# First batch of an attention-and-experts kernel: row sums from a second, crosswise product, and its last two head pairs side by side

## The chip, the cores and the metric

The kernel runs on one NeuronCore of a Trainium2 chip. The metric is the device time in microseconds (us) of one execution, median of several runs. An engine's work is issued in program order on that engine's own queue: TensorE (PE) multiplies and transposes, VectorE (DVE) and ScalarE (ACT) do elementwise work, GpSimd (POOL) does slower elementwise work, and SyncE (SP) issues the DMA transfers.

## What is computed

Three layers follow each other over 8 batches of 576 tokens with 8 heads of 64 (512 columns a token):

```python
kv  = einsum('bhsd,bhse->bhde', k, v)          # per head 64 x 64
out = einsum('bhsd,bhde->bhse', q, kv)
x   = out / sqrt(mean(out*out, -1) + 1e-6) * g_norm     # per head
xn  = x / sqrt(mean(x*x, -1) + 1e-6) * rms_g            # per token
y   = (silu(xn @ w_gate) * (xn @ w_val)) @ w_out        # 512 -> 1536 -> 512
# then: each token goes to the best of 8 experts (512 -> 1024 -> 512)
```

The scale of a token therefore needs, for each of its 8 heads, the sum of the squares of `out` over 64 columns, and the same sum weighted with g_norm squared.

## The kernel before, in words

The order of the work is written out by hand: the program's order is the order on each engine's queue, and waits between engines follow from the data. The work comes in nine chunks of 512 tokens (chunk 0 is the first 512 tokens of batch 0). In chunk 0 the gated layer is also fed: its float64 weights are loaded as pairs of 32-bit words and turned into float32 and then into a high and a low part (class `Convert`: `rebias` L909 on ACT, `narrow` L922, L923, L926 on DVE, `high` L949 on ACT, `low` L959 on DVE). A raw weight buffer comes free for the next load when `narrow` is through.

The change lies in the opening, L1470 to L1509, ahead of the first product of the gated layer. Heads go in four pairs. For each pair of batch 0:
- `column` (L672) copies k or q into an order with the token in the partition; k's copies are on DVE, q's on ACT.
- `kv` (L678) multiplies k and v (20 products of 64 columns a pair, L691) and copies the two 64 x 64 blocks of the result into `kvb`, one on DVE (L692), one on ACT (L693).
- `turn` (L695) transposes q on PE (four transposes, L703); ACT copies the result out of PSUM (L705).
- `av` (L708) makes four products of 128 columns (L715): tokens in the partitions, the pair's 128 columns along the row. ACT squares it (L719) and copies it to `xo` (L720); POOL multiplies the squares with g squared (`sg`, L737); DVE sums both over 64 columns (L741, one for the squares, one for `sg`).

`finish` (L757) turns the sums into a scale per token and head with seven small DVE instructions (L761 to L767), `root` (L771) takes the square root on ACT, ACT then loads the table for Silu (L1504), `scale` (L775) scales `xo` for one head pair at a time on DVE (L777), and `tstep` (L840) transposes it (L844), makes the high part on ACT (L848) and the low part on DVE (L849). The products of the gated layer (L154 to L156) start with the first of them.

In the opening, pairs 0 and 1 are loaded alone, pairs 2 and 3 together (`krest`, `vrest`, `qrest`), and behind them on SP's queue come four weight loads, with g_norm (`gcol`, L127 and L128) and rms_g between the first and the second, and then batch 1. The pairs are taken one after the other (L1478 to L1488). While DVE and ACT end the batch, PE does 56 transposes of the identity that nobody reads (L1498 and L1499).

Of the kernel before, what the change touches and what calls it, by code (L numbers as in the profile page):

```python
# [10 lines left out]
F32 = mybir.dt.float32  # L11
F32R = mybir.dt.float32r
# [3 lines left out]
ALU = mybir.AluOpType  # L16
# [4 lines left out]
P = 128  # L21
# [44 lines left out]
def attention_moe_kernel(ctx, tc, q, k, v, g_norm, w_gate, w_val, w_out, rms_g, wg2, w1, w2, out):  # L66
# [267 lines left out]
    class Block:  # L334
# [47 lines left out]
        def turn(self, t):  # L382
            m = self.rows[t]
            ps = ptile(f"tr{self.nm}_{t}")
            for kk in range(KD):
                nc.tensor.transpose(
                    ps[:, kk * P : kk * P + m], self.xg[t][:m, kk * P : kk * P + P], ident[:m, :m]
                )
            p3 = ps.rearrange("p (k t) -> p k t", k=KD)[:, :, :m]
            sl = slice(t * P, t * P + m)  # L390
            if not self.slots:
                split(self.whole[0][:, :, sl], self.whole[1][:, :, sl], p3)
                return
            for i in range(2):
                split(self.xh[i][:, :, sl], self.xl[i][:, :, sl], p3[:, 2 * i : 2 * i + 2])
# [218 lines left out]
    class Attention:  # L614
# [54 lines left out]
                    q[self.b - 1 + i, :, 512:S, :].rearrange("h s d -> s h d"),  # L669
                )  # L670

        def column(self, nm, hp, copy=nc.scalar.copy):  # L672

            t = att.tile([P, 4, 2, HD], F32, tag="col", bufs=2, name=f"{nm}c{self.b}_{hp}")
            copy(t, self.t[hp][nm].rearrange("p h j d -> p j h d"))
            self.col[nm, hp] = t.rearrange("p j h d -> p j (h d)")

# [14 lines left out]
            nc.vector.tensor_copy(kb[0:64, h0 : h0 + n, 0:64], pt[0:64, 0:n, 0:64])  # L692
            nc.scalar.copy(kb[64:128, h0 : h0 + n, 64:128], pt[64:128, 0:n, 64:128])  # L693

        def turn(self, hp):  # L695
            self.sums()
            ps = self.ps(f"qT{self.b}_{hp}")
            for j in range(4):
                if hp < 4:
                    src = self.col["q", hp][:, j, :]  # L700
                else:
                    src = x5[:, 2 * j : 2 * j + 2, :].rearrange("p h d -> p (h d)")
                nc.tensor.transpose(ps[:, j * P : j * P + P], src, ident)  # L703
            qT = att.tile([P, 4, P], F32, tag="qT", bufs=2, name=f"qTs{self.b}_{hp}")
            nc.scalar.copy(qT.rearrange("p a b -> p (a b)"), ps)  # L705
            self.qTs.append(qT)

        def av(self, hp, apart=False):  # L708
# [48 lines left out]
        def finish(self):  # L757
            self.sums()
            n = self.n
            a1, a2, m2 = s1[:, :n, :], s2[:, :n, :], st[:, :n]  # L760
            nc.vector.tensor_scalar(a1, a1, 1.0 / HD, EPS, op0=ALU.mult, op1=ALU.add)  # L761
            nc.vector.reciprocal(a1, a1)
            nc.vector.tensor_tensor(a2, a2, a1, op=ALU.mult)
            nc.vector.tensor_reduce(m2, a2, axis=AX.X, op=ALU.add)
            nc.vector.tensor_scalar(m2, m2, 1.0 / D, EPS, op0=ALU.mult, op1=ALU.add)
            nc.vector.reciprocal(m2, m2)
            nc.vector.tensor_tensor(  # L767
                a1, a1, m2[:, :, None].to_broadcast([P, n, 8]), op=ALU.mult
            )
# [20 lines left out]
        def steps(self, nxt, tight=False):  # L790


            def kv(h):
                self.kv(h, h + 1)
                for hp in (h, h + 1):
                    self.column("q", hp)
                if h == 0:
                    self.load(2, 3)
                else:
                    if self.n == 5:  # L800
                        self.load_last()
                    if nxt:
                        nxt.load(0, 1)

            def turn(h):
                for hp in (h, h + 1):
                    self.turn(hp)
                for hp in (0, 1):
                    if h == 0:
                        self.column("k", hp + 2)  # L810
                    elif nxt:
                        nxt.column("k", hp)

            def av(h):
                for hp in (h, h + 1):
                    self.av(hp, tight)

            res = []
            if self.b == 1:
                res += [idle, lambda: self.column("k", 0), lambda: self.column("k", 1), idle]  # L820
            for h in (0, 2):
                for f, kind in ((kv, "p"), (turn, "p"), (av, "a")):
                    res += [mark(kind, lambda f=f, h=h: f(h)), idle]
                if tight:
                    res[-1] = mark("v", lambda: self.squares())
            if self.n == 5:
                res += [mark("p", lambda: self.turn(4)), idle]
                res += [mark("a", lambda: self.av(4, tight)), idle]
                if tight:
                    res[-1] = mark("v", lambda: self.squares())  # L830
            res += [idle] * (1 if tight else 2)
            res += [mark("f", self.finish), idle, mark("t", self.root)]
            if self.n == 5:
                res.append(mark("v", self.scale_last))
            step = 2 if tight else 1
            for kk in range(0, KD, step):
                res.append(mark("v", lambda kk=kk: [self.scale(kk + i) for i in range(step)]))
            return res

    def tstep(c, kk):  # L840

        ps = (otile if (c, kk % 2) == (0, 1) else ptile)(f"xT{c}_{kk}")
        for j in range(4):
            nc.tensor.transpose(ps[:, j * P : j * P + P], xo[:, j, kk * P : kk * P + P], ident)  # L844
        if kk == 3:
            live[0] -= xt[kk] is not None
        x = (rslot if c < SINGLE and kk < 3 else wslot)(f"x{c}_{kk}")
        nc.scalar.activation(x[:, 0:512], ps, AF.Copy, scale=comb[:, kk : kk + 1])  # L848
        nc.vector.scalar_tensor_tensor(  # L849
            x[:, 512:1024], ps, comb[:, kk : kk + 1], x[:, 0:512].bitcast(F32),  # L850
            op0=ALU.mult, op1=ALU.subtract,
        )
        xt[kk] = x
# [621 lines left out]
    small_loads()  # L1475
    for _ in range(3):
        conv.load()
    for hp in range(4):  # L1478
        a0.column("k", hp, vec)
        if hp == 1:  # L1480
            nc.vector.tensor_tensor(g2b, g2b, g2b, op=ALU.mult)
        if hp > 1:
            a0.av(hp - 2)
        a0.column("q", hp)
        a0.kv(hp)
        if hp == 3:
            conv.rebias()
        a0.turn(hp)  # L1488
    a1.load(0, 1)
    late_loads()  # L1490
    conv.narrow()
    a0.av(2)
    a0.av(3)
    conv.high()
    conv.rebias()

    unread = otile("unread")
    for i in range(56):  # L1498
        nc.tensor.transpose(unread[:, 0:P], ident, ident)  # L1499
    a0.finish()  # L1500
    nc.vector.tensor_scalar(comb, comb, gcol[:, 0:1], None, op0=ALU.mult)
    conv.low()
    a0.root()
    nc.scalar.activation(warm, warm, AF.Silu)  # L1504
    for kk in range(KD):
        a0.scale(kk)
    tstep(0, 0)
    tstep(0, 1)
    conv.narrow()  # L1509

    def tstep_kk(kk):
# [704 lines left out]
```

## Time and profile before

| | us |
|---|---|
| median of 3 runs | 1455.35 |
| lowest and highest | 1452.74 and 1456.58 |
| the profiled execution | 1455.73 |
| its span, first to last instruction | 1454.1 |

The profile follows one execution. Times in it count from the start of the span. A row of the timeline has start, duration, engine, line, operation, what is written and read, the count, and in brackets how long the engine stood idle before it and what released it. "PEclk" is the share of TensorE's full clock that was granted (1.00 is 2.4 GHz, 0.50 is 1.2 GHz). Busy times of PE are modelled from pipelined instructions; a mean of one can be longer than its pace in a row of equal ones.

### The profile page before, as it was taken

The page shows a single profiled execution, that of the slowest core. Times are in us where ns is not written, and L with a number is a line of the kernel's source. Part 1 is how long each engine was busy: PE and PEld are TensorE (multiplying, and loading weights), DVE is VectorE, ACT ScalarE, POOL GpSimd, SP SyncE. Part 2 cuts the span into 40 slices and gives each one's busy share as a digit, 9 for nine tenths or more (in the row PEclk, how much of TensorE's full clock was granted, in tenths as well). Part 3 has the DMA queues.
Part 4 walks back from the last instruction along what each step waited for, and adds up shares of the span by engine and source line. Part 5 has one row for each costly group of instructions (what it writes and reads, how often), then busy time and mean ns, then how long its engine had stood idle before and what let it go on. Part 6 is the DMA issues. An engine that isn't in the chain of part 4 may idle for free.

```text
span 1454.1 us, 21584 instructions
## 1 busy us (share of the span) xinstructions
PE 1422.5 (98%) x7844; PEld 1196.3 (82%) x7844; DVE 928.9 (64%) x1970; ACT 629.8 (43%) x1173; POOL 198.5 (14%) x207
## 2 busy tenths in 40 slices
PE   6999999999999999999999999999999999999997
PEld 5776778888888888887888888788999989988985
DVE  5989675695677554665557446844462778578661
ACT  4655433433444544344222332243333556556651
POOL 2010001011012010101000100121404212302111
PEclk9999999999999999999999999999999999999999
DMA  7776856665666686558657555764323334424320
GB/s 218 247 220 215 277 167 173 212 219 152 209 212 177 204 272 192 174 167 280 241 191 212 178 190 198 219 213 122 131 81 99 106 127 141 134 93 134 119 84 30
DMA packets 162860, 255.55 MB, mean 176 GB/s; under 512 B 27331, under 2 KB 93123, under 8 KB 162752
## 3 DMA queue, kind: packets, MB, share of 16 engines
q1 hardware_dynamic: 131264, 190.26, 41.1%
q10 hardware_dynamic: 23040, 44.05, 9.4%
q0 software_dynamic: 8448, 19.85, 4.1%
q8 instruction: 63, 1.03, 0.3%
q14 instruction: 45, 0.37, 0.1%
HBM read 199.68 MB, written 55.30 MB: 175 GB/s over the span
## 4 chain that ended last, share of the span: by engine, by line
PE 85%; DVE 6%; DMA 5%; issue 3%; ACT 1%; SPq 1%; POOL 0%; POOLq 0%; ACTq 0%; DVEq 0%
PE A L1258 8%; PE X L1258 6%; PE po L154 6%; PE po L155 6%; PE po L156 6%; PE pv L154 3%; PE pv L155 3%; PE pv L156 3%; PE pg L154 3%; PE pg L155 3%; PE pg L156 3%; PE av L715 1%; PE kv L691 1%; DMA k<-in_k 1%; PE qT L703 1%
## 5 line engine op out<-in xcount | busy, mean ns | idle before, releaser
L1023 DVE SCALAR_TENSOR_TENSOR junk<-x,wgb 128x512 bf16<-128x512 f32 x256 | 183.0, 715 | 5.0
L154 PE MATMUL po<-wo,ahl 128*128 128x512 f32 x408 | 161.0, 395 | 0.9 <-DVE x L1001 0.9
L155 PE MATMUL po<-wo,ahl 128*128 128x512 f32 x408 | 159.0, 390 | 0.0
L156 PE MATMUL po<-wo,ahl 128*128 128x512 f32 x408 | 159.0, 390 | 0.0
L1258 PE MATMUL A<-xp,r 128*128 128x512 f32 x504 | 130.4, 394 | 1.9 <-DVE X L1834 1.3
L1258 PEld LDWEIGHTS A<-xp,r 128*128 128x128 f32 x504 | 93.1, 188 | 22.5 <-DVE X L1834 2.2
L737 POOL TENSOR_TENSOR sg<-sq,g2b 128x512 f32<-128x512 f32 x36 | 48.9, 1359 | 421.5 <-ACT sq L719 348.5
L1096 POOL DMA_INDIRECT idxd<-rec,si x36 | 38.3, 1064 | 458.6 <-DVE cs L1105 347.9
L1258 PE MATMUL X<-xp,r 128*128 128x512 f32 x360 | 93.3, 394 | 0.2 <-ACT X L1825 0.2
L154 PEld LDWEIGHTS po<-wo,ahl 128*128 128x128 f32 x408 | 76.6, 188 | 17.2 <-DVE x L1001 1.4
L156 PEld LDWEIGHTS po<-wo,ahl 128*128 128x128 f32 x408 | 76.6, 188 | 16.3
L155 PEld LDWEIGHTS po<-wo,ahl 128*128 128x128 f32 x408 | 76.7, 188 | 15.4
L1258 PEld LDWEIGHTS X<-xp,r 128*128 128x128 f32 x360 | 66.4, 188 | 14.8 <-ACT X L1825 0.9
L154 PE MATMUL pv<-x,wv 128*128 128x512 f32 x192 | 76.8, 400 | 0.7 <-DVE sl L1895 0.7
L154 PE MATMUL pg<-x,wg 128*128 128x512 f32 x192 | 77.1, 402 | 0.1
L155 PE MATMUL pg<-x,wg 128*128 128x512 f32 x192 | 75.2, 391 | 2.0 <-DVE wg L959 2.0
L155 PE MATMUL pv<-x,wv 128*128 128x512 f32 x192 | 75.4, 392 | 1.1 <-DVE wv L959 1.1
L156 PE MATMUL pg<-x,wg 128*128 128x512 f32 x192 | 75.1, 391 | 0.9 <-DVE x L849 0.9
L156 PE MATMUL pv<-x,wv 128*128 128x512 f32 x192 | 75.0, 391 | 0.0
L1896 ACT ACTIVATE ahl<-sl 128x512 fp32r<-128x512 f32 x42 | 26.5, 631 | 103.1 <-DVE sl L1895 100.2
L250 ACT ACTIVATE wo<-re 128x512 fp32r<-128x512 f32 x84 | 51.1, 627 | 31.8 <-DVE re L261 31.2
L253 DVE TENSOR_TENSOR wo<-re,wo 128x512 fp32r<-128x512 f32 x84 | 56.5, 684 | 9.5 <-ACT wo L250 9.1
(813 smaller groups left out, 3377.8 us busy)
## 6 DMA issues: line engine op xcount, KB each, us to landing
wo<-wos SPq DMA_DIRECT2D x90, 512.0 KB
r<-wst ACTq DMA_DIRECT2D x72, 512.0 KB
re<-in_moe_w SPq DMA_DIRECT2D x64, 512.0 KB
x1d<-x SPq DMA_DIRECT2D x32, 256.0 KB
k<-in_k SPq DMA_DIRECT2D x30, 256.0 KB
v<-in_v SPq DMA_DIRECT2D x30, 256.0 KB
q<-in_q SPq DMA_DIRECT2D x30, 256.0 KB
rg<-in_moe_w_gate SPq DMA_DIRECT2D x12, 512.0 KB
```

Of the source, the lines that this page charges most:

```text
L154: nc.tensor.matmul(ps, lhi, rhi, start=first, stop=False)
L155: nc.tensor.matmul(ps, llo, rhi, start=False, stop=False)
L156: nc.tensor.matmul(ps, lhi, rlo, start=False, stop=last)
L250: nc.scalar.activation(w[:, 0], part(n), AF.Copy)
L253: nc.vector.tensor_tensor(w[:, 1], part(n), w[:, 0].bitcast(F32), op=ALU.subtract)
L691: nc.tensor.matmul(pt[o, c, o], kj, vj, start=j == 0, stop=j == 4)
L703: nc.tensor.transpose(ps[:, j * P : j * P + P], src, ident)
L737: nc.gpsimd.tensor_tensor(sg, sq3, g2b[:, None, :].to_broadcast([P, 8, HD]), op=ALU.mult)
L1023: nc.vector.scalar_tensor_tensor(j, self.rows[t], 1.0, wgb[e], op0=ALU.mult, op1=ALU.mult, accum_out=self.L[:, t, e : e + 1],)
L1096: nc.gpsimd.indirect_dma_start(out=idxd[:], out_offset=bass.IndirectOffsetOnAxis(ap=si[:, j : j + 1], axis=0), in_=rec[:, j, :], in_offset ...
L1258: nc.tensor.matmul(ps, w[:, a, kk, :], x[kk][b], start=first and kk == j == 0, stop=kk == 1 and j == 2, skip_group_check=True,)
L1896: nc.scalar.activation(ahl[:, 0:512], sl, AF.Copy)
```

## The change

A class `Early` takes over the end of batch 0. For each pair, `across` makes the same product a second time the other way round: one product of 512 columns with the pair's 128 columns in the partitions and the tokens along the row. ACT squares that. `sums` multiplies the squares, 128 tokens at a time, by a 128 x 4 matrix `sel` (two columns of ones, two of g_norm squared, one of each for each head), so that TensorE makes both sums for both heads and leaves them in PSUM (`S`). `along` is the old product, copied to `xo` by ACT. `weigh` builds `sel` on POOL from `gcol`. DVE's sums (L741) and POOL's `sg` (L737) are gone from batch 0; the other batches keep them.

Pairs 2 and 3 are taken together: both columns of k, then q of pair 2 on DVE and of pair 3 on ACT, one `kv` for both, then `turn` for 2 (copied out by ACT) and for 3 (copied out by DVE). They have buffers of their own (`more`, `turned`). The unread transposes go from 56 to 6. `conv.low` moves from ahead of the root to behind the first `scale`, and scales 1 to 3 are issued between the steps of `tstep`.

```diff
--- before.py
+++ after.py
@@ -669,9 +669,10 @@
                     q[self.b - 1 + i, :, 512:S, :].rearrange("h s d -> s h d"),
                 )
 
-        def column(self, nm, hp, copy=nc.scalar.copy):
-
-            t = att.tile([P, 4, 2, HD], F32, tag="col", bufs=2, name=f"{nm}c{self.b}_{hp}")
+        def column(self, nm, hp, copy=nc.scalar.copy, t=None):
+
+            if t is None:
+                t = att.tile([P, 4, 2, HD], F32, tag="col", bufs=2, name=f"{nm}c{self.b}_{hp}")
             copy(t, self.t[hp][nm].rearrange("p h j d -> p j h d"))
             self.col[nm, hp] = t.rearrange("p j h d -> p j (h d)")
 
@@ -692,7 +693,7 @@
             nc.vector.tensor_copy(kb[0:64, h0 : h0 + n, 0:64], pt[0:64, 0:n, 0:64])
             nc.scalar.copy(kb[64:128, h0 : h0 + n, 64:128], pt[64:128, 0:n, 64:128])
 
-        def turn(self, hp):
+        def turn(self, hp, copy=nc.scalar.copy, qT=None):
             self.sums()
             ps = self.ps(f"qT{self.b}_{hp}")
             for j in range(4):
@@ -701,8 +702,9 @@
                 else:
                     src = x5[:, 2 * j : 2 * j + 2, :].rearrange("p h d -> p (h d)")
                 nc.tensor.transpose(ps[:, j * P : j * P + P], src, ident)
-            qT = att.tile([P, 4, P], F32, tag="qT", bufs=2, name=f"qTs{self.b}_{hp}")
-            nc.scalar.copy(qT.rearrange("p a b -> p (a b)"), ps)
+            if qT is None:
+                qT = att.tile([P, 4, P], F32, tag="qT", bufs=2, name=f"qTs{self.b}_{hp}")
+            copy(qT.rearrange("p a b -> p (a b)"), ps)
             self.qTs.append(qT)
 
         def av(self, hp, apart=False):
@@ -757,10 +759,15 @@
         def finish(self):
             self.sums()
             n = self.n
-            a1, a2, m2 = s1[:, :n, :], s2[:, :n, :], st[:, :n]
+            a1, a2 = s1[:, :n, :], s2[:, :n, :]
             nc.vector.tensor_scalar(a1, a1, 1.0 / HD, EPS, op0=ALU.mult, op1=ALU.add)
             nc.vector.reciprocal(a1, a1)
             nc.vector.tensor_tensor(a2, a2, a1, op=ALU.mult)
+            self.means()
+
+        def means(self):
+            n = self.n
+            a1, a2, m2 = s1[:, :n, :], s2[:, :n, :], st[:, :n]
             nc.vector.tensor_reduce(m2, a2, axis=AX.X, op=ALU.add)
             nc.vector.tensor_scalar(m2, m2, 1.0 / D, EPS, op0=ALU.mult, op1=ALU.add)
             nc.vector.reciprocal(m2, m2)
@@ -836,6 +843,64 @@
             for kk in range(0, KD, step):
                 res.append(mark("v", lambda kk=kk: [self.scale(kk + i) for i in range(step)]))
             return res
+
+    class Early:
+
+
+        def __init__(self, a):
+            self.a, self.q = a, []
+            self.sel = cpool.tile([P, 4], F32, name="gsel")
+            self.S = psg.tile([P, 512], F32, tag="v", name="S0")[:, 0:64].rearrange(
+                "p (j h i) -> p j h i", j=4, h=4
+            )
+            nc.gpsimd.memset(self.sel, 0.0)
+
+        def weigh(self):
+            for i in range(2):
+                o = slice(64 * i, 64 * i + 64)
+                nc.gpsimd.memset(self.sel[o, i : i + 1], 1.0)
+                nc.gpsimd.tensor_tensor(
+                    self.sel[o, 2 + i : 3 + i], gcol[o], gcol[o], op=ALU.mult
+                )
+
+        def across(self, hp):
+            qT = self.a.qTs[hp]
+            ps = ptile(f"aT{hp}")
+            nc.tensor.matmul(
+                ps, kvb[0][:, hp, :], qT.rearrange("p a b -> p (a b)"), start=True, stop=True
+            )
+            sq = att.tile([P, D], F32, tag="tmp", bufs=3, name=f"sqT{hp}")
+            nc.scalar.activation(sq, ps, AF.Square)
+            self.q.append(sq)
+
+        def sums(self, hp):
+            for j in range(4):
+                nc.tensor.matmul(
+                    self.S[:, j, hp, :], self.q[hp][:, j * P : j * P + P], self.sel,
+                    start=True, stop=True,
+                )
+
+        def along(self, hp):
+            qT, ps = self.a.qTs[hp], otile(f"av0_{hp}")
+            for j in range(4):
+                nc.tensor.matmul(
+                    ps[:, j * P : j * P + P], qT[:, j, :], kvb[0][:, hp, :], start=True, stop=True
+                )
+            nc.scalar.copy(
+                xo[:, 0:4, hp * P : hp * P + P], ps.rearrange("p (j e) -> p j e", e=P)
+            )
+
+        def finish(self):
+            a1, a2 = s1[:, 0:4, :], s2[:, 0:4, :]
+            p1, p2 = (
+                t.rearrange("p j (h i) -> p j h i", i=2) for t in (a1, a2)
+            )
+            nc.vector.tensor_scalar(
+                p1, self.S[:, :, :, 0:2], 1.0 / HD, EPS, op0=ALU.mult, op1=ALU.add
+            )
+            nc.vector.reciprocal(a1, a1)
+            nc.vector.tensor_tensor(p2, self.S[:, :, :, 2:4], p1, op=ALU.mult)
+            self.a.means()
 
     def tstep(c, kk):
 
@@ -1475,37 +1540,61 @@
     small_loads()
     for _ in range(3):
         conv.load()
-    for hp in range(4):
+    early = Early(a0)
+    for hp in range(2):
         a0.column("k", hp, vec)
         if hp == 1:
             nc.vector.tensor_tensor(g2b, g2b, g2b, op=ALU.mult)
-        if hp > 1:
-            a0.av(hp - 2)
         a0.column("q", hp)
         a0.kv(hp)
-        if hp == 3:
-            conv.rebias()
         a0.turn(hp)
+    early.weigh()
+    more, turned = (
+        wpool.tile([P, 1024], F32R, tag="w", bufs=NSLOT, name=f"more{i}").bitcast(F32)
+        for i in range(2)
+    )
+    more = more.rearrange("p (c j h d) -> p c j h d", c=2, j=4, h=2)
+    turned = turned.rearrange("p (c j t) -> p c j t", c=2, j=4)
+    a0.column("k", 2, vec)
+    a0.column("k", 3, vec, more[:, 0])
+    early.across(0)
+    early.along(0)
+    early.across(1)
+    a0.column("q", 2, vec)
+    a0.column("q", 3, t=more[:, 1])
+    a0.kv(2, 3)
+    a0.turn(2, qT=turned[:, 0])
+    early.sums(0)
+    early.sums(1)
+    conv.rebias()
+    a0.turn(3, vec, turned[:, 1])
     a1.load(0, 1)
     late_loads()
     conv.narrow()
-    a0.av(2)
-    a0.av(3)
+    early.across(2)
+    early.across(3)
+    early.along(1)
+    early.sums(2)
+    early.sums(3)
     conv.high()
     conv.rebias()
+    early.along(2)
+    early.along(3)
 
     unread = otile("unread")
-    for i in range(56):
+    for i in range(6):
         nc.tensor.transpose(unread[:, 0:P], ident, ident)
-    a0.finish()
+    early.finish()
     nc.vector.tensor_scalar(comb, comb, gcol[:, 0:1], None, op0=ALU.mult)
-    conv.low()
     a0.root()
     nc.scalar.activation(warm, warm, AF.Silu)
-    for kk in range(KD):
-        a0.scale(kk)
+    a0.scale(0)
+    conv.low()
+    a0.scale(1)
     tstep(0, 0)
+    a0.scale(2)
     tstep(0, 1)
+    a0.scale(3)
     conv.narrow()
 
     def tstep_kk(kk):
```

## Rows read from the trace of the kernel before

**Rows 1.** The page's part 4: shares of the chain that ended last, by engine.
```profile
PE 85%; DVE 6%; DMA 5%; issue 3%; ACT 1%; SPq 1%; POOL 0%; POOLq 0%; ACTq 0%; DVEq 0%
```

**Rows 2.** Busy time by stretch: stretch, length, engines (instructions), clock, DMA share, GB/s.
```profile
32.00:41.50 9.50, 7.42 (x33) 5.01 (x33) 9.30 (x18) 5.79 (x11) 0.00 (x0) 1.00 0.31 99
41.50:79.00 37.50, 37.48 (x229) 28.20 (x230) 32.60 (x56) 24.11 (x46) 3.10 (x3) 1.00 0.78 250
```

**Rows 3.** The chain in order of time, up to 90 us: start, us, what.
```profile
7.70 10.19 DMA rg<-in_moe_w_gate
...
50.73 1.32 PE kv L691 x40
...
81.97 7.85 DMA rw<-in_moe_w_out
```

**Rows 4.** Timeline, 11 to 17 us: a load issued, and two loads' first readers.
```profile
11.32 0.83 SPq L128 DMA_DIRECT2D gcol<-in_g_norm  x1
...
13.24 0.43 DVE L675 COPY kc<-krest 128x512 f32<-128x512 f32 x1 [1.95 <-DMA krest<-in_k]
...
16.25 0.62 ACT L675 COPY qc<-qrest 128x512 f32<-128x512 f32 x1 [1.68 <-DMA qrest<-in_q]
```

**Rows 5.** Timeline, 21 to 26 us: the last pair is turned; ACT behind it.
```profile
21.36 0.65 PE L703 MATMUL qT<-ident,qc 128*128 128x128 f32 x4 [0.58 <-ACT qc L675]
...
22.27 0.58 ACT L705 COPY qTs<-qT 128x512 f32<-128x512 f32 x1
...
23.00 0.60 ACT L719 ACTIVATE sq<-av 128x512 f32<-128x512 f32 x1
...
25.60 0.69 ACT L909 ACTIVATE cmv<-rv 128x512 f32<-128x512 f32 x1
```

**Rows 6.** Timeline, 27 to 37 us: from the sums to the gated layer.
```profile
27.36 0.19 DVE L761 TENSOR_SCALAR s<-s 128x32 f32<-128x32 f32 x1
...
28.95 0.23 DVE L1501 TENSOR_SCALAR comb<-comb,gcol 128x4 f32<-128x4 f32 x1
29.06 0.23 ACT L773 ACTIVATE s<-s 128x32 f32<-128x32 f32 x1 [2.78 <-DVE s L767]
...
29.31 1.28 ACT L1504 ACT_TABLE_LOAD   x1
29.69 2.49 DVE L777 TENSOR_TENSOR xo<-xo,s 128x512 f32<-128x512 f32 x4
...
31.86 0.19 PEld L154 LDWEIGHTS pg<-x,wg 128*128 128x128 f32 x1 [0.35 <-ACT x L848]
...
33.42 0.41 DVE L922 TENSOR_SCALAR cmv<-cmv 128x512 int32<-128x512 int32 x1
...
35.20 1.40 DVE L849 SCALAR_TENSOR_TENSOR x<-xT,comb,x 128x512 fp32r<-128x512 f32 x2
```

**Rows 7.** Groups by line and shape, 0 to 32 us: count | busy us, mean ns | idle.
```profile
L1499 PE MATMUL unread<-ident 128*128 128x128 f32 x56 | 6.3, 273 | 0.0
...
L737 POOL TENSOR_TENSOR sg<-sq,g2b 128x512 f32<-128x512 f32 x4 | 5.5, 1365 | 16.7 <-ACT sq L719 15.0 <-issue 1.6
...
L741 DVE TENSOR_REDUCE s<-sq 128x8 f32<-128x512 f32 x4 | 2.7, 684 | 4.0 <-ACT sq L719 4.0
...
L122 POOL CAST kw<-kw8i 128x32 f32<-128x32 int32 x1 | 0.2, 219 | 0.1
```

**Rows 8.** Groups of DVE by line and shape over the whole span.
```profile
L1001 DVE COPY x<-po 128x512 f32<-128x512 f32 x18 | 12.2, 687 | 14.2 <-PE po L156 14.1
```

**Rows 9.** The chain again: eight products of 512 columns in float32, at 47 us.
```profile
47.29 3.43 PE po L1942 x8
```

**Rows 10.** Busy time by stretch around the falls of the clock, columns as in rows 2.
```profile
13.60:17.00 3.40, 0.88 (x21) 0.78 (x22) 1.90 (x5) 1.69 (x4) 1.27 (x1) 1.00 1.08 306
17.00:20.40 3.40, 3.40 (x26) 3.18 (x28) 0.06 (x1) 1.37 (x4) 0.00 (x0) 0.50 1.01 323
...
24.00:30.40 6.40, 6.18 (x57) 5.94 (x55) 5.51 (x16) 3.58 (x7) 3.93 (x10) 1.00 0.96 193
```

## The prediction

> **What bounds the kernel now.** I read the chain of waits first. Over the whole span it is 85% PE [rows 1], but the change touches only the first 37 us, so that stretch decides. By stretches [rows 2], from 32.0 to 41.5 us DVE is busy 9.30 of 9.50 us and PE 7.42: the gated layer starts under DVE, which makes both x's low parts and the weights. From 41.5 to 79 us PE is full (37.48 of 37.50). No transfer in these stretches has a fixed hour: each weight load waits for a raw buffer that DVE's `narrow` frees, so an earlier start moves all of it forward. What has a fixed hour are the opening's loads, which SP issues from the first microsecond. krest is there at 13.24 us and qrest at 16.25 [rows 4]; the first weights, rg, at 7.70 + 10.19 = 17.89 us [rows 3].
>
> After qrest the old opening is a row of steps: two pairs after one another, PE at half clock from 17.0 to 20.4 [rows 10], the last pair turned at 21.36 and copied by 22.85 [rows 5], then its squares, POOL's last `sg`, a last sum, and `finish` from 27.36. Root at 29.06, scales from 29.69, the first gated product's weights at 31.86, `narrow` from 33.42, the last two low parts from 35.20 [rows 6]. `narrow` at 33.42 is the mark to beat: from there DVE has no gap worth the name.
>
> **What is removed.** Eight sums at 0.68 us on DVE and four `sg` at 1.37 us on POOL [rows 7]. Only the last `sg` and the last sums were on the path. The 50 transposes that go are 50 x 6.3/56 = 5.6 us of PE that nobody waits for; they cost time only through the clock (below).
>
> **The new opening, step by step.** Where the same instruction stands in the trace, its duration is used.
> - kv of pairs 2 and 3: 40 products in a row take 1.32 us [rows 3]; with krest copied twice by about 14.1 and vrest between krest and qrest (about 14.7), they end by 16.5. q is then last: DVE copies pair 2 from 16.25 in 0.43 (k's copy [rows 4]), ACT pair 3 in 0.62. So kv of pair 3 leaves the path.
> - turn of pair 2: 16.7 to 17.35 (0.65 [rows 5]), ACT's copy to about 17.95.
> - **`sums` of pairs 0 and 1** stand next on PE, ahead of turn 3, and need `sel`, which needs `gcol`. Its second half was issued at 11.32 [rows 4], behind rg on the same queue. If the queue lands in order, it comes after 17.89: I take 18.2. POOL's two last small instructions at 0.2 (the 128x32 cast takes 0.22 [rows 7]) give 18.6. PE, in order, waits from 17.35 to 18.6 with turn 3 queued behind: a new wait of 1.25 us. Bounds: no wait at all, if these few bytes overtake rg; upwards, gcol's first reader stands at 28.95 [rows 6], and POOL's instructions can't cost more than the 1.37 us of a `sg` [rows 7]. Rg's end is the nearer row, since it lies just ahead on the same queue.
> - One `sums` instruction pair (load 128 columns, multiply 4): no such shape is shown. An unread transpose goes at 6.3/56 = 0.11 us [rows 7] and has the same load; I take 0.11, between 0.03 (a 64-column kv product, 1.32/40) and 0.19 (one LDWEIGHTS [rows 6]). Eight: 0.9, to 19.5.
> - turn 3 to 20.15; DVE copies it out of PSUM. Price: 0.69, a copy of that size from PSUM [rows 8]; done 20.9.
> - `across` is one product of 512 columns, 3.43/8 = 0.43 us [rows 9]. Pair 2's hides in front of that copy; pair 3's is out by 21.55. ACT squares it until 22.2 (0.6, like the copies of rows 5). `along` 1 and the first four `sums` lie beside that; the last four add 0.45: `S` is ready at 22.85.
> - DVE's `narrow` (1.86 us, 33.42 to 35.28 [rows 6]) is queued ahead of `finish`, but starts at 20.9 and ends at 22.75. It costs nothing; without that cover `finish` would wait for it.
> - `finish` to root takes 29.06 - 27.36 = 1.70 [rows 6]; its operands now come partly from PSUM, which I price at nothing to 0.2. Root could start at 24.55. On ACT, `high` stands ahead of it and waits for `narrow` (22.75), with `rebias` and two copies of `xo` behind it. ACT's five starts after 23.00 reach 25.60, a pace of 0.52 [rows 5]: four from 22.8 end near 24.9 to 25.0, so root goes at **25.0**, against 29.06: 4.1 us earlier.
> - Behind the root some is given back. The first product stood 31.86 - 29.06 = 2.8 us behind the root [rows 6]; now scale 0 no longer waits for `low`, and the table load (1.28) with the first high part (0.7) sets it: about 27.4, 2.4 us behind. On DVE, however, `low` is no longer in the root's shadow, and DVE waits about 0.3 us for that high part. Scale 0 at 25.3, then `low`, scale 1 (2.49/4 = 0.62 each scale, 0.7 a low part [rows 6]) to 27.2, the wait to 27.5, then low part, scale, low part, scale give `narrow` at **30.15**. PE's two transposed blocks and ACT's high parts lie beside that.
>
> Sum: 33.42 - 30.15 = **3.3 us**. The weights need nothing earlier than they land: batch 1's loads and the first four weights stay on the same SP queue in the same order. 1455.73 of the profiled execution less 3.3 is 1452.4; the median is 0.4 lower, so 1452.0. Bounds of the single terms: `sel` on time gives 1.25 more; dearer `sums` (0.19) take 1.0 of it; ACT's tail (0.45) may or may not count. I hold a gain of 2.0 to 4.4 likely.
>
> **Rivals.**
> 1. *The clock falls.* From 13.6 to 17.0 PE was busy 0.88 of 3.40 us, and from 17.0 to 20.4 the granted clock was 0.50, that is 1.2 GHz; with the 56 unread transposes PE was busy 6.18 of 6.40 us from 24.0 to 30.4, at 1.00 [rows 10]. In the new opening PE has little to do from about 24.3 (6 unread transposes) to 27.4. A like fall there lasts 3.4 us if it is as long as that one, and delays PE by at most half of it, 1.7; DVE's queue covers part. Time: up to 1453.7. For it: the gap. Against: two transposed blocks lie in it, and DVE, not PE, sets the pace behind it [rows 2]. Chance 0.12. The Trainium skill, TensorE: Matmul & The Clock Gate, on the HAM clock gate, says that the throttled clock is the default and that an idle stretch brings it back, which speaks against taking the 50 transposes out; by that rule the time is this rival's, and the trace agrees that the clock falls after a thin stretch.
> 2. *The opening is shorter than summed.* gcol is four bytes a row and may land before rg's last part, and then turn 3 goes at 17.35. That gives 3.3 + 1.25, 1450.8; its first reader at 28.95 [rows 6] doesn't tell. Chance 0.24.
> 3. *The gain is absorbed.* The chain passes a weight load of 7.85 us at 81.97 [rows 3]; such a load met by other traffic could take the gain back. Against: it is itself released by DVE, so it comes earlier too. Time 1455. Chance 0.08.
> 4. *Slower: PE stands before `sums`.* Everything of pair 3 is queued behind that wait. It gives the whole gain back if `sel` comes 3.3 us later than summed, at 21.9. Four POOL instructions at the price of a `sg`, 1.37 [rows 7], behind 18.2 end at 23.7: 1.8 slower than before, 1457.2. With gcol as late as its first reader allows (28.95) and POOL cheap, `sel` would come 10.8 later, 7.5 slower than before: 1462.9. Against: POOL's 128x32 cast takes 0.22, and these have one column. Chance 0.06.
>
> **How the numbers follow.** Forecast 0.50, rivals 0.12, 0.24, 0.08 and 0.06. A difference under 0.3%, 4.4 us, can't be told from none for this kernel. The forecast and rivals 1 and 3 lie within it. Rival 2 gives 4.55, at the bound; with the upper half of the forecast's spread (run to run the kernel moves by 3.8 us) I give faster 0.27, slower 0.06, of rival 4 and that spread. The range leaves out 2 in 10: from 1449.2, rival 2 (1450.8) less 1.6 for the spread of a median of such runs, to 1455.2, just past rival 3.
>
> **What would show it.** Right: qT 3 copied by DVE near 20 to 21 us, `S` complete near 23, root near 25, the first gated weights near 27.4, `narrow` near 30.2, and the same distance from there to 79 and 147 us as before. PE idle before `sums` with POOL as its releaser confirms the wait on gcol; PE going on without a stop at 17.4 is rival 2. A granted clock of 0.50 after 24 us is rival 1. The forecast is wrong if root comes after 27, if DVE waits for PE between 27 and 41, or if the gain stands at 40 us and is gone at 147.

## The result, and the profile after

The changed kernel takes 1468.76 us (median of 6 runs, 1465.43 to 1470.69), against 1455.96 us of the kernel before on the same chip (6 runs, 1452.74 to 1457.63): a ratio of 1.0087, with a 95% interval of 1.0073 to 1.0102. It is 12.8 us slower. The forecast was 1452.0, the range ended at 1455.2. The profiled execution of after took 1465.43 us, the lowest of its six, with a span of 1463.6.

The chain of waits after, page part 4 (answers to rows 1):

```profile
PE 87%; DVE 5%; DMA 3%; issue 3%; ACT 1%; SPq 0%; ACTq 0%; POOL 0%; POOLq 0%; DVEq 0%
```

More of the chain is PE than before. The chain of after in order of time (start, us, what) shows where, the opening first:

```profile
11.07 1.12 PE qT L704 x4
12.18 1.71 PE aT L869 x2
13.89 1.71 PE av L886 x8
15.60 1.31 PE aT L869 x2
16.91 1.32 PE kv L692 x40
18.23 0.59 PE qT L704 x4
18.81 1.82 PE S L878 x16
20.63 0.49 PE qT L704 x4
21.12 1.91 PE aT L869 x4
23.04 0.89 PE av L886 x8
23.93 1.68 PE S L878 x16
25.61 1.90 PE av L886 x16
...
80.96 8.40 DMA rw<-in_moe_w_out
...
146.93 3.44 PE po L2031 x8
...
515.67 10.34 DMA k<-in_k
...
1453.17 4.03 DMA out_dram<-yo7a,idx7a
```

The chain of before: two pieces of its opening, then the same later pieces (the one at 81.97 is in rows 3):

```profile
17.95 4.40 DMA k<-in_k
...
25.44 1.30 POOL sg L737
...
147.35 3.44 PE po L1942 x8
...
514.35 9.98 DMA k<-in_k
...
1443.20 4.42 DMA out_dram<-yo7a,idx7a
```

Two things are to be read here. From 11.07 to 27.51 us the chain never leaves PE, where before it went through DMA, DVE and POOL: **the opening has become PE's**. And the loss is not in it. After stands 1.01 us ahead at 81 us and 0.42 ahead at 147, then falls behind: 1.32 us at 514, 9.97 at 1443. It is lost long after the changed lines, little by little, where PE is full.

The timeline of after, 12 to 37 us (columns as in rows 4), with the rows that answer to rows 5 and 6:

```profile
13.68 1.92 PE L886 MATMUL av<-kvb,qTs 128*128 128x128 f32 x8
...
18.04 0.19 POOL L862 TENSOR_TENSOR gsel<-gcol 64x1 f32<-64x1 f32 x1 [13.43 <-DMA gcol<-in_g_norm]
...
22.87 1.05 PE L886 MATMUL av<-kvb,qTs 128*128 128x128 f32 x8
...
25.65 0.19 DVE L898 TENSOR_SCALAR s<-S 128x32 f32<-128x32 f32 x1 [2.01 <-PE S L878]
...
26.64 0.59 ACT L889 COPY xo<-av 128x512 f32<-128x512 f32 x1 [1.01 <-PE av L886]
...
27.54 0.59 ACT L889 COPY xo<-av 128x512 f32<-128x512 f32 x1 [0.31 <-PE av L886]
...
28.02 0.23 ACT L780 ACTIVATE s<-s 128x32 f32<-128x32 f32 x1
...
30.68 0.19 PEld L154 LDWEIGHTS pg<-x,wg 128*128 128x128 f32 x1
...
32.98 0.42 DVE L987 TENSOR_SCALAR cmv<-cmv 128x512 int32<-128x512 int32 x1
```

The root stands at 28.02 (29.06 before), the first gated weights at 30.68 (31.86) and `narrow` at 32.98 (33.42) [rows 6]. So the new opening is 0.44 us ahead in this pair of executions, not 3.3. Even that is not a gain shown: the start of `narrow` moves from execution to execution. In the profiles of the nine kernels below and above that have the opening of before it lies between 31.6 and 33.6 us (33.0 in the middle), in the four that have the opening of after between 33.0 and 36.4.

Where are the 10 us lost? Busy time by stretch (columns as in rows 2), first of all engines, then of the instructions of one tile alone: of `y5a`, the second layer of one expert (120 products of 512 columns), and of `po` (the gated layer's output) from 500 to 1020 us. After:

```profile
12.00:28.00 16.00, 16.00 (x127) 12.36 (x126) 5.49 (x16) 8.39 (x16) 2.27 (x12) 1.00 1.04 293
1000.00:1454.00 454.00, 453.31 (x2664) 402.64 (x2663) 272.94 (x532) 224.18 (x479) 97.26 (x101) 1.00 0.32 106
...
1300.00:1460.00 160.00, 28.02 (x120) 21.25 (x120) 1.50 (x2) 2.06 (x3) 0.99 0.27 93
...
500.00:1020.00 520.00, 186.23 (x729) 136.60 (x729) 8.08 (x12) 6.74 (x12) 1.00 0.63 203
```

Before:

```profile
1000.00:1454.00 454.00, 443.36 (x2622) 397.65 (x2620) 271.94 (x530) 222.90 (x476) 99.55 (x102) 0.99 0.32 105
...
1300.00:1460.00 160.00, 27.38 (x120) 21.28 (x120) 1.50 (x2) 2.06 (x3) 0.97 0.27 90
...
500.00:1020.00 520.00, 183.58 (x729) 136.54 (x729) 8.08 (x12) 6.74 (x12) 1.00 0.63 202
```

The same 120 products keep PE busy 28.02 us instead of 27.38, the same 729 recorded ones of `po` 186.23 instead of 183.58. PE waits for nothing and its clock is full. **Each product has become slower**: by 0.64/120 = 5.3 ns and by 2.65/729 = 3.6 ns. The "mean ns" of a group is not this pace: for `y5a` it is 389 ns in before and 395 in after, longer than the step from one product to the next, since the durations of pipelined products overlap. The pace shows in the starts. In the chain of before, 49 products of `y5a` in a row start from 1329.91 to 1340.79 us, one each 10.88/48 = 226.7 ns; in that of after 48 start from 1339.88 to 1350.79, one each 10.91/47 = 232.1 ns.

From the starts of all recorded pairs of neighbours with 512 columns, before and after: 227.7 and 232.5 ns for the experts' second layers (`y`, 984 products), 227.5 and 230.1 for `po` (1272), 227.6 and 228.8 for the gated layer's first products (`pg` and `pv`, 1440), 228.2 and 229.4 for the same products in chunks 4 to 7, where they are made in another form (tiles `A` and `X`, 1008). Times their counts that is 4.7 + 3.3 + 1.7 + 1.2 = 10.9 us, about what the chain lost between 33 us and the end (9.97 + 0.44 = 10.4). Nothing of the diff is in these products. What can reach them is where their operands lie: the new tile `sel` has 16 bytes a partition, takes 32 of `cpool`, and everything allocated behind it, all weight slots among them, stands 32 bytes higher (byte 14944 of a partition instead of 14912). The pools at the upper end of SBUF, which hold `ahl` and `wo` for `po` and the hidden tiles `hs` for `y`, stay where they were. For `y` and `po` one operand has so moved against the other. The last two kinds, 2.9 of the 10.9 us, have both operands on the side that moved; the last section comes back to them.

The trace holds a comparison of its own. `y0a` is the one second layer whose hidden tiles lie in weight slots, so that both its operands moved together; those of `y0b`, which comes next, lie in an upper pool. Busy time of their 48 products each from 1000 to 1100 us (columns as in rows 2, `y0a` first), before:

```profile
1000.00:1100.00 100.00, 11.32 (x48) 8.87 (x48) 1.38 (x2) 1.00 0.29 94
...
1000.00:1100.00 100.00, 11.33 (x48) 8.87 (x48) 1.38 (x2) 1.00 0.29 94
```

After:

```profile
1000.00:1100.00 100.00, 11.35 (x48) 8.87 (x48) 1.38 (x2) 1.00 0.31 96
...
1000.00:1100.00 100.00, 11.62 (x48) 8.86 (x48) 1.38 (x2) 1.00 0.31 96
```

`y0a` keeps its pace and `y0b` loses it. The work of other engines is not what slows `y`: the pairs during which DVE, ACT and POOL were all idle go at 226.9 ns in before (180 pairs) and at 232.1 in after (191), and the share of DMA from 1000 to 1454 us is 0.32 in both.

### The profile page after: what moved, and what is told of

The parts are those of the page before. It is cut to its first block, busy times and chain, and to the rows that moved or that the text cites. A ratio compares the mean times of both kernels' runs of the same rounds, so it can differ in the third digit from the quotient of the medians.

```text
span 1463.6 us, 21550 instructions
## 1 busy us (share of the span) xinstructions
PE 1434.7 (98%) x7834; PEld 1194.9 (82%) x7834; DVE 924.7 (63%) x1963; ACT 629.3 (43%) x1170; POOL 193.3 (13%) x208
## 4 chain that ended last, share of the span: by engine, by line
PE 87%; DVE 5%; DMA 3%; issue 3%; ACT 1%; SPq 0%; ACTq 0%; POOL 0%; POOLq 0%; DVEq 0%
PE A L1323 8%; PE X L1323 6%; PE po L154 6%; PE po L156 6%; PE po L155 6%; PE pv L154 3%; PE pv L155 3%; PE pv L156 3%; PE pg L154 3%; PE pg L156 3%; PE pg L155 3%; PE av L717 1%; PE kv L692 1%; PE qT L704 1%; DMA k<-in_k 1%
## 5 line engine op out<-in xcount | busy, mean ns | idle before, releaser
L739 POOL TENSOR_TENSOR sg<-sq,g2b 128x512 f32<-128x512 f32 x32 | 43.7, 1366 | 413.2 <-ACT sq L721 329.5
L155 PEld LDWEIGHTS po<-wo,ahl 128*128 128x128 f32 x408 | 76.7, 188 | 16.4
```

Source lines behind the costliest of these rows:

```text
L155: nc.tensor.matmul(ps, llo, rhi, start=False, stop=False)
L739: nc.gpsimd.tensor_tensor(sg, sq3, g2b[:, None, :].to_broadcast([P, 8, HD]), op=ALU.mult)
```

## Experiments on the place of the operands

**16 bytes alone.** The kernel before, with a tile of that size that nobody reads:

```diff
     for _ in range(3):
         conv.load()
+    pad = cpool.tile([P, 4], F32, name="pad")
+    nc.gpsimd.memset(pad, 0.0)
```

> The kernel before, with one unused tile of 16 bytes a partition added to the first pool, which moves the weight slots, x and the attention tiles up by 32 bytes (from byte 14912 to 14944 of a partition) and leaves the tiles at the right end where they were. Theory (the changed kernel is slower because the new tile sel moves these addresses, so that 512-column products go at 230 ns instead of 228): 1463 to 1469 us, loss spread over the whole span from 200 us on, products of the experts' second layer near 232 ns from start to start instead of 227. Rival (the loss comes from the opening, the slots' new order or the swapped PSUM banks): 1455 to 1457, products at 227.

Measured: 1465.61 us against 1455.59, ratio 1.0069 [1.0052, 1.0085]. Busy time by stretch of `y5a` and of `po` in it:

```profile
1300.00:1460.00 160.00, 28.02 (x120) 21.24 (x120) 1.50 (x2) 2.06 (x3) 0.99 0.28 93
...
500.00:1020.00 520.00, 186.19 (x729) 136.59 (x729) 8.08 (x12) 6.74 (x12) 1.00 0.64 203
```

They are those of after. One unread tile of 16 bytes costs 10.0 of the 12.8 us.

**A second tile, so that the slots move by 64.** The changed kernel with the same `pad`:

> The changed kernel, with a second small tile behind sel, so that the slots start at byte 14976, again a multiple of 64. Theory of the addresses: the whole loss goes and the opening's gain is left, 1454 to 1456.5 us, products at 227 to 228 ns. Rival (slots' order, banks, fewer unread transposes, work of the opening): 1466 to 1470, as the changed kernel.

Measured: 1465.57, ratio 1.0065 [1.0048, 1.0082]; `y5a` busy 27.72 us for its 120. A multiple of 64 doesn't bring the pace back. That version of the theory falls; the time is just under the rival's range, and the pace lies between those of before and after.

**The other allocations of the change.** The kernel before with two more weight slots taken at the start (as `more` and `turned` do) and the tile `S0` ahead of the others in its PSUM pool:

```diff
+    turn0 = psg.tile([P, 512], F32, tag="v", name="S0")
+    nc.vector.memset(turn0[:, 0:4], 0.0)
+    more, turned = (
+        wpool.tile([P, 1024], F32R, tag="w", bufs=NSLOT, name=f"more{i}").bitcast(F32)
+        for i in range(2)
+    )
```

> The kernel before, with the two extra weight slots and with the PSUM tile v taken before g, so that the two swap banks as in the changed kernel; no address moves by 32 bytes. Theory of the addresses: 1455 to 1457 us. Rival (banks or slots): 1463 to 1469.

Measured: 1455.3, ratio 1.0001 [0.9992, 1.0011], `y5a` 27.38. Turning the slots and the banks costs nothing.

**Both operands moved, but apart.** `pad` as above, and 32 bytes at the head of the two upper pools, which grow downwards:

```diff
+        if c == 1:
+            padr = ap1.tile([P, 8], F32, name="padr")
+            nc.gpsimd.memset(padr, 0.0)
...
+    pads = sbb.tile([P, 8], F32, name="pads")
+    nc.gpsimd.memset(pads, 0.0)
```

> As the kernel before with 16 bytes more in the first pool, and 32 bytes more in the two pools at the right end as well (32 bytes lower), so that both operands of every product lie 32 bytes off a multiple of 64. If it is the two operands' place against each other that counts (one on a multiple of 64, the other off it): back to 1455 to 1458 us. If each operand off a multiple of 64 costs by itself: 1466 us or more, and the products of chunks 1 to 3, whose tiles all moved, slower too.

Measured: 1462.35, ratio 1.0042 [1.0026, 1.0059]; `y5a` busy 27.58 us for its 120.

Neither expectation was met. The edit did another thing than its name says: the lower pools go up by 32 and the upper ones down by 32, so the distance between the two operands of a product changes by 64, as it does in the second experiment, where only the slots moved. Both have the same paces (`y` 229.1 ns, `po` 229.4). That pointed to the **distance** between the operand that is streamed and the one that is loaded.

**Only one side, of one kind of product.** The kernel before with the hidden tiles alone 32 bytes lower:

```diff
+    pads = sbb.tile([P, 8], F32, name="pads")
+    nc.gpsimd.memset(pads, 0.0)
     xops.extend(xslots)
```

> The kernel before, in which only the pool with the experts' hidden tiles (hs, the weights that PE loads for the second layer) lies 32 bytes lower; w2, which streams against them, stays. About 980 products read such a pair. Theory (the two operands' places against each other set the pace): only these products go at 232 ns instead of 227, all others as before, and the time grows by 980 x 5.5 ns = 5.4 us to about 1461. Rival (the absolute place of the streamed operand counts): 1455 to 1457, 227 ns.

Measured: 1461.07 (9 runs) against 1455.66, ratio 1.0032 [1.0022, 1.0043], 5.4 us. `y5a` and `po` in it:

```profile
1300.00:1460.00 160.00, 28.03 (x120) 21.25 (x120) 1.50 (x2) 2.06 (x3) 0.97 0.27 90
...
500.00:1020.00 520.00, 183.63 (x729) 136.55 (x729) 8.08 (x12) 6.75 (x12) 1.00 0.64 203
```

The products of the tile that moved are slow, by starts 232.5 ns instead of 227.7; `po` is as before, and so is `y0a` (11.32 us for its 48, against 11.62 for those of `y0b`). 984 products by 4.8 ns are 4.7 us, inside the interval (3.2 to 6.3 us).

**Both sides moved together.** The kernel before with every operand of the products 32 bytes higher: a small tile of the router is moved from the pools at the upper end into `cpool`.

```diff
+    n1c = cpool.tile([1, 8], F32, name="n1c")
+    nc.gpsimd.memset(n1c, 0.0)
...
-        n1, g8, r8, i8 = t1("n1", [8]), t1("g8", [8, 8]), t1("r8", [8]), t1("i8", [48])[:, 0:8]
+        n1, g8, r8, i8 = n1c, t1("g8", [8, 8]), t1("r8", [8]), t1("i8", [48])[:, 0:8]
...
-        nf, i8, sel, npos = t1("nf", [8]), t1("i8f", [8]), t1("sel", [8, 8]), t1("npos", [8])
+        nf, i8, sel, npos = sba.tile([1, 8], F32, name="nf"), t1("i8f", [8]), t1("sel", [8, 8]), t1("npos", [8])
```

> The kernel before with every tile behind the first constants 32 bytes higher: the slots (14944), x, and the tiles of both pools at the right end (one small tile each is moved to the left side, so that these pools begin 32 bytes higher). The places of the operands against each other are as before. Theory (the distance between two operands counts): 1455 to 1457 us, products at 226 to 228 ns as before. Rival (each operand's own place counts, a multiple of 64): 1464 to 1467, as with 16 bytes in the first pool alone.

Measured: 1455.27 against 1455.02, ratio 1.0002 [0.9993, 1.0011]:

```profile
1300.00:1460.00 160.00, 27.41 (x120) 21.28 (x120) 1.50 (x2) 2.06 (x3) 0.97 0.27 90
...
500.00:1020.00 520.00, 183.60 (x729) 136.54 (x729) 8.08 (x12) 6.75 (x12) 1.00 0.64 203
```

Here the weight slots stand at the very byte at which they stand in after, and the products are as fast as before. So it isn't the place of an operand by itself that costs, it is its distance from something that stayed. For `y` the experiment before this one and `y0a` show that this is the product's other operand; for `po` no run moved an operand of its alone.

**Which distances.** The whole lower side 128 bytes up (`pad` of 32 words), and the hidden tiles alone 512 and 256 bytes lower (`pads` of 128 and of 64 words):

> The kernel before with an unused tile of 128 bytes in the first pool: slots at byte 15040, that is 128 bytes on. The products of the experts' second layer went at 226.5 ns at an offset of 0, 232.5 at 32 and 228.5 at 64. If the pattern repeats every 128 bytes: 1455 to 1457 us and 227 ns. If any move away from the present place costs: 1461 us or more and 229 ns or more.

> As the run in which only the experts' hidden tiles were moved, but by 512 bytes in place of 32. The products of the second layer went at 227 ns at a distance of 0, 232 to 233 at 32, 228 to 230 at 64, 232 at 128. If the pattern repeats within 512 bytes: 227 ns and 1455 to 1457 us. If every move costs: 229 ns or more, 1457.5 or more.

> The same by 256 bytes. If the pattern repeats within 256 bytes: 227 ns and 1455 to 1457 us; otherwise 229 ns or more and 1457.5 or more.

Measured: 128 bytes, 1461.72, ratio 1.0045 [1.0028, 1.0062]; 512 bytes, 1455.31, ratio 0.9998 [0.9988, 1.0008]; 256 bytes, 1454.45, ratio 0.9995 [0.9986, 1.0005]. The row of `y5a` at 128 bytes:

```profile
1300.00:1460.00 160.00, 28.00 (x120) 21.34 (x120) 1.50 (x2) 2.06 (x3) 0.98 0.27 90
```

All together, by how far the distance differs from that of the kernel before (`y` by starts, lowest and highest mean of the eight experts; `y5a` busy for 120 products):

| distance moved, bytes | a `y` product, ns | `y5a` busy, us | kernels |
|---|---|---|---|
| 0 | 226.7 to 229.9 | 27.38 to 27.41 | before, 32 bytes up on both sides, slots and banks |
| 32 | 231.3 to 233.3 | 28.02 to 28.03 | after, 16 bytes, hidden tiles alone |
| 64 | 228.5 to 230.5 | 27.58 to 27.72 | two tiles, moved apart |
| 128 | 231.1 to 233.2 | 28.00 | 128 bytes |
| 256, 512 | 226.7 to 229.9 | 27.38 | hidden tiles by 256, by 512 |

This is the order for `y`. `po` has another: 227.5 ns at 0, 230.1 at 32, 229.4 at 64, 228.5 at 128.

## Experiments on the opening

**The change without its 16 bytes.** `sel` in the unused part of the 32 bytes that `gcol` takes anyway, so that nothing else moves:

```diff
-    gcol = const([P, 1], F32, "gcol")
+    gcol5 = const([P, 5], F32, "gcol")
+    gcol = gcol5[:, 0:1]
...
-            self.sel = cpool.tile([P, 4], F32, name="gsel")
+            self.sel = gcol5[:, 1:5]
```

> The changed kernel with sel in the 32 bytes that gcol takes anyway, so that no tile behind it moves (slots at byte 14912, as before). Everything else of the change is there. Theory of the addresses: the loss goes as a whole, and the opening's gain of 0.4 us at narrow is left: 1454 to 1456.5, products at 227. Rival (something else of the change also costs: unread transposes, slots, banks, order): over 1459.

Measured: 1457.73 (10 runs, 1453.63 to 1461.55) against 1455.66, ratio 1.0012 [1.0001, 1.0023]. All later paces are those of before (`y5a` 27.38). The 10 us are gone, and what is left is the opening itself: 2.1 us slower in the median. With the 10.0 of the 16 bytes alone that makes 12.1 of the 12.8 us. The paces are those that the theory expected; the time lies between the two expectations and meets neither. The timeline of its profiled execution (1458.48 us):

```profile
13.28 1.05 PE L887 MATMUL av<-kvb,qTs 128*128 128x128 f32 x8
...
18.46 2.45 PE L879 MATMUL S<-gcol,sqT 128*128 128x4 f32 x16 [1.36 <-POOL gcol L863]
...
21.66 3.62 PE L870 MATMUL aT<-more,kvb 128*128 128x512 f32 x4
...
35.89 0.42 DVE L988 TENSOR_SCALAR cmv<-cmv 128x512 int32<-128x512 int32 x1
```

And its busy time by stretch:

```profile
20.00:22.00 2.00, 2.00 (x10) 1.99 (x10) 0.10 (x1) 0.00 (x0) 0.44 (x3) 0.50 1.07 351
```

Here PE does stand 1.36 us before `sums`, with POOL as its releaser, and after that the granted clock is 0.50, 1.2 GHz, from 19.72 to 26.55 us, in a stretch that belongs to PE: four `aT` rows take 3.62 us, 2.07 in the profile of after. `narrow` comes at 35.89, 2.5 us later than before [rows 6], and the span is 2.6 us longer. In the profiled execution of after PE reached `sums` too late to wait, and the clock was 1.00 from 16.4 us on. So the opening goes in more than one way from run to run, and the profile of after is of its fastest run.

**The same with gcol ahead of the bulk.** The two transfers of `gcol` are issued before `krest`:

```diff
     def small_loads():
-        nc.sync.dma_start(gcol[0:64, :], g_norm.rearrange("(e o) -> e o", o=1))
-        nc.sync.dma_start(gcol[64:128, :], g_norm.rearrange("(e o) -> e o", o=1))
...
+    nc.sync.dma_start(gcol[0:64, :], g_norm.rearrange("(e o) -> e o", o=1))
+    nc.sync.dma_start(gcol[64:128, :], g_norm.rearrange("(e o) -> e o", o=1))
     a0.load_rest()
```

> The changed kernel with sel in gcol's 32 bytes, and gcol's two transfers issued ahead of krest. In the run with sel in gcol PE stood 1.36 us before the sums with POOL as its releaser, the clock fell at 19.9 us and stayed at 0.50 until 26.7, and finish began at 28.56. Theory (that wait, and the fall behind it, are what takes the opening's gain back): no wait on POOL, PE goes from turn 2 into the sums at about 17.1, no long fall of the clock, finish begins near 24 to 25, narrow of the second weights before 33.0, time 1453 to 1455.5. Rival (the sums themselves, 2 us for two pairs, are the opening's bound): finish near 26 and 1455 to 1457.

Measured: 1453.73 (12 runs) against 1455.02, ratio 0.9997 [0.9988, 1.0006]. The wait is gone, the gain isn't there. Timeline:

```profile
18.18 1.95 PE L877 MATMUL S<-gcol,sqT 128*128 128x4 f32 x16
...
26.53 0.19 DVE L897 TENSOR_SCALAR s<-S 128x32 f32<-128x32 f32 x1 [2.93 <-PE S L877]
...
33.86 0.42 DVE L986 TENSOR_SCALAR cmv<-cmv 128x512 int32<-128x512 int32 x1
```

`sums` start without a releaser at 18.18 (krest's copy now began at 14.19 instead of 13.07, behind the two transfers), yet the sums are complete only at 26.53: PE's own work is the bound, as the rival had it, part of it at half clock. The time is in the theory's range, but `finish` and `narrow` (33.86, expected before 33.0) are the rival's. The clock fell here as well (0.50 from 19.78 to 23.19 us), without any wait on POOL. So this run doesn't price the wait apart from the clock, and the fall is not shown to come from that wait. It is the best form of the change found, and no measurable gain over the kernel before.

**The clock alone.** The kernel before with 6 unread transposes instead of 56:

```diff
-    for i in range(56):
+    for i in range(6):
         nc.tensor.transpose(unread[:, 0:P], ident, ident)
```

> The kernel before with 6 unread transposes in place of 56. Rival 1 of the prediction (the clock falls in the gap and PE is late for the gated layer): the granted clock shows 0.50 for some 3.4 us behind 26 us, and the time is up to 1.7 us longer, 1456 to 1457.5. Theory that these transposes matter nothing: 1455 to 1456.5 and no fall.

Measured: 1455.03 (10 runs) against 1455.66, ratio 0.9998 [0.9988, 1.0007]. Busy time by stretch:

```profile
26.00:28.00 2.00, 0.00 (x0) 0.00 (x0) 1.79 (x9) 0.00 (x0) 1.03 (x7) 1.00 0.74 86
...
30.00:32.00 2.00, 2.00 (x9) 1.44 (x7) 1.87 (x3) 1.31 (x2) 0.00 (x0) 0.50 0.42 148
```

PE does nothing from 24 to 28 us, and the clock is at 0.50 behind it, from 28.35 to 35.17 us (in before it was 1.00 from 24.0 to 30.4 [rows 10]). The fall is that of the first rival, but it costs nothing that can be measured: DVE, busy 1.87 of 2.00 us, sets the pace there.

## Why the prediction was wrong

**The step that failed** is the first: "the change touches only the first 37 us, so that stretch decides". No term and no rival let the rest of the kernel change its pace. The profile of before gave no ground for taking that pace as fixed: `A` and `X` products with an operand in the attention tiles go at 232 to 235 ns in it (112 pairs), and `y4a` at 229.9, next to 226.7 to 228 for their neighbours. A new constant of 16 bytes moved one operand of the later products by 32 bytes against the other, and that costs 10.0 us in a kernel whose code is otherwise the same. The mark named for it, "the same distance from there to 79 and 147 us as before", was set too near: from `narrow` to the weight load at 81 us it is 47.98 us after and 48.55 before, at 147 us after is still 0.42 us ahead, and the loss comes behind that. Of the marks for a miss, a root after 27 us is met (28.02), but it tells of the opening alone.

**The opening: no gain is shown, where 3.3 us were forecast.** `narrow` is 0.44 us earlier in the one profile of after, and in the median after's opening alone is 2.1 us slower. By its terms:

- *A row was taken for a product.* A float32 product stands as two rows in the trace: one `across` is two rows, the eight `sums` of two pairs are sixteen. The eight rows at 47.29 [rows 9] are four products, so `across` costs 0.96 (1.91 for two on the chain) and not 0.43, and eight `sums` 1.82 and 1.68, not 0.9. (The 20 rows of a pair's `kv`, called products there, are likewise ten.) The transposes from which 0.11 was taken are one row each. The upper bound, 0.19 for each of the `sums`, was too low as well: 1.82/8 = 0.23.
- *PE's clock.* The sum takes the new opening's PE rows at full clock, without a term for less. In after `across` 0, `along` 0 and `across` 1 fill PE from 12.18 to 16.91, and `kv` for pairs 2 and 3 ends at 18.23, not 16.5. These rows run at half their later pace: eight rows of `av` take 1.92 us at 13.68 and 1.05 at 22.87. The trace of after has its first entry of the granted clock at 16.4 us, and the 1.00 shown ahead of it stands for no entry. With `sel` in `gcol`'s bytes the entries begin at 12.9 us, the same eight rows take 1.05 us at 13.28, and `kv` ends at 16.5 as summed. So the early rows of after ran at the lower level, 1.2 GHz (the last section has the other profiles). Where the full clock came early, it fell to 0.50 again amid the `sums`, at 19.7 to 19.8 us (`finish` from 28.56 and, with `gcol` loaded early, from 26.53); where it came late, it did not (25.65).
- *The end of the sums.* 25.65 instead of 22.85. Of these 2.8 us 1.7 are there when `kv` ends, by the clock. From there the row takes 7.4 us instead of 6.35, although the wait of 1.25 on `gcol` fell away in after: the dearer `across` and `sums` more than fill it.
- *ACT's tail.* It was to set the root at 25.0 by a pace of 0.52. In after its two last copies wait for PE's last products (1.01 and 0.31 us in the timeline). The root comes at 28.02; ACT is only the end of PE's row.
- *From the root on* the step was right: `narrow` 4.96 us behind the root, 5.15 predicted.

**Right.** `sel` was ready at 18.63 (18.6 predicted, gcol behind rg), the wait on it was 1.36 us where PE came early enough (1.25 predicted). `narrow`'s three instructions ahead of `finish` are hidden: DVE waited 2.01 us for the sums.

**Rivals.** The first, a fall of the clock where the transposes go, is not what happened: after shows 1.00 from 16.4 to 32 us, and the experiment with 6 transposes shows that the fall, when it comes there, costs nothing. The rule by which these transposes were worth keeping (the Trainium skill, TensorE: Matmul & The Clock Gate, HAM clock gate) agrees with the trace on the clock and not on the time. Where a fall does cost is in PE's row of `sums`, from 19.7 us on, and no rival had it there. The second, a shorter opening, is excluded by gcol's landing. The fourth, slower by a late `sel`, has the sign right and the mechanism wrong: `sel` was late by no more than summed. The wait that the sum had, together with the fall of the clock, is the likeliest reading of the 2.1 us that are left without the shift: with `gcol` loaded early the ratio is 0.9997 instead of 1.0012. It is not shown, since the two intervals overlap and each form of the opening has one profile.

## What to carry to other kernels

Before a change is priced by its own stretch, look at what it allocates: compare the addresses of every operand with those of before, and put a small new constant into unused bytes, as here in `gcol`'s, or pad it so that distances stay (the padding was not run). A slow drift over a stretch that nobody edited, at full clock and with no new wait, is a pace, and it is read from the starts of equal products, not from their modelled durations. Count rows, not products, when a float32 product is priced from a trace, and look where the entries of the clock begin before a 1.00 is believed.

## What was not expected of the hardware

In the experts' second layer the pace of a product of 512 columns changes with the distance in SBUF between its two operands: 226.7 to 229.9 ns at the distance of before and with the hidden tiles 256 or 512 bytes lower, 231.3 to 233.3 at 32, 228.5 to 230.5 at 64, 231.1 to 233.2 at 128. The Trainium skill, SBUF — State Buffer, section "SBUF: two separate sides", says in a passage on contention between engines that PE never waits on anyone. The trace agrees as far as other engines go (`y` is slow, at 232.1 ns, with all of them idle too); these runs show a cost that comes with PE's own two operands.

Why it does stays open, and so do 2.9 of the 10.9 us: the gated layer's first products, both of whose operands moved together, lost 1.2 ns each in after and none when everything moved. The trace shows where they lost it. The first six `pg` and `pv` products behind a `po` went from 226.9 to 230.0 ns (318 pairs), the seventh and later ones from 227.0 to 227.6 (500). `po` itself has most of its loss there too: 227.9 to 231.2 ns for the first six behind another kind (671 pairs), 227.0 to 228.2 for the later ones (381). `y` is slow all along its rows. Whether a product's pace hangs on where the operands of the products just ahead of it lie was not tested. Distances other than these were not tried, nor the change with `sel` padded to 256 bytes.

The early products of both kernels ran at half their later pace (1.92 and 1.05 us above) while the clock's column shows 1.00, since it has no entry there yet: the first one stands at 13.6 us in before, at 16.4 in after, at 12.9 in the run with `sel` in `gcol`'s bytes. In the nine profiles in which eight such rows (`av` of pair 0) end ahead of the first entry they take 1.91 or 1.92 us, in the three in which they start with it or behind it 1.05 to 1.07. So ahead of its first entry the clock was at the lower level, 1.2 GHz. Why it rose earlier in one execution than in another is not shown.
